# A hand-ordered attention and gated-convolution kernel: new table generation, the filter sent through the batches' own DFT, and a new order of every step

## The chip, the cores and the metric

One core of a Trainium2 chip. A core has five engines with queues of their own: TensorE (PE: matrix multiplications into PSUM, and the loads of their weights), VectorE (DVE), ScalarE (ACT), GpSimd (POOL) and SyncE (SP), which here only issues transfers. The metric is the device time of one execution in microseconds, lower is better; several runs are made and their median is taken.

## The reference, cut to what matters

Random-feature linear attention for 8 batches of 8 heads with 576 positions of 64 features; its output is a batch of 576 x 512, which goes through a gated long convolution.

```
def phi(x):
    proj = einsum('bhsd,df->bhsf', x, w_phi)              # 64 -> 128 features
    proj = proj - max(abs(proj), axis=-1, keepdims=True)
    return concatenate([exp(proj), exp(-proj)], axis=-1)
q_p, k_p = phi(q), phi(k)
kv  = einsum('bhsf,bhsd->bhfd', k_p, v);  z = sum(k_p, axis=2)
att = einsum('bhsf,bhfd->bhsd', q_p, kv) / (einsum('bhsf,bhf->bhs', q_p, z) + 1e-6)
x = att of all heads side by side                         # 8 x 576 x 512
x1, x2, x3 = split(x @ w_proj, 3)                         # 512 -> 3 * 512
x2c = irfft(rfft(x2, axis=1) * rfft(filter, axis=0), axis=1)
out = (x1 * x2c * x3) @ w_out                             # 512 -> 512
```

## The kernel before

Everything is a step, a short method of the class `Kernel`, and the order of all steps is written out by hand in the string `PLAN` (lines 26 to 186): `run` (line 997) takes its words one by one and emits each step's instructions. A word such as `Fe,ACT,0,2@6` is a step's name, its engine where it has a choice, batch and part, and the first of its PSUM banks. Every engine has its own queue and works through it strictly in the order in which the words put its instructions there; what a step needs from another engine it waits for, and everything behind it on its queue waits too. PSUM has eight banks, and a step reuses a bank as soon as its last reader is done. SBUF buffers that turn over have two to four copies (`RING`, line 22; `at`, line 216, picks the copy by an index).

The steps of a batch `b`, with `v` for a block of two heads and `X` for half of them:

- `load`, `loadh` (lines 560, 566): GpSimd issues the transfers of q, k, v into `qn`, `kn`, `vn`, cast to bf16. `trh` (line 573): SyncE issues a transposing transfer of half of it into `qT` or `kT`. For batch 0 TensorE transposes instead (`pt`, line 580) and `pte` (line 586) copies out.
- `Pk`, `Qn` (lines 597, 604), with `Pkt`, `Qnt` for the leftover positions: projections by w_phi. `maxk`, `maxq` (lines 681, 685), `maxkt`, `maxqt`: VectorE takes the maxima of the absolute values. `ex`, `exkt`, `exqt` (lines 656 to 675): ScalarE exponentiates with both signs. `mhi`, `mlo`, `trm`, `trme` prepare q's maxima as rows; `Pq`, `Pqt` (lines 628, 645) project q the other way round and subtract them.
- `em`, `vs` (lines 713, 718): v is weighted by the exponential of k's maximum, on GpSimd. `KV`, `KVe` (lines 724, 738): k's features times v, 72 matmuls a half, and the copy out. `NE`, `NEt` (lines 742, 752): q's features times that. `rc`, `xn`, `rct`, `xnt` (lines 761 to 784): VectorE divides.
- `trx`, `trxt` (lines 786, 791): SyncE issues transposing transfers of the attention output into `xT`, `xTt`; `ptx`, `ptxt` do it on TensorE for batch 0.
- `f1`, `f2` (lines 815, 821): two levels of folding by sums and differences, which make a 576-point transform into smaller ones; mostly on GpSimd. `F` (line 826): the folded DFT of the attention output by TensorE; each result has 2 x 288 columns (even and odd frequencies, cosine and sine), of which 128 + 128 go out by `Fe` (line 837) and 32 leftover ones of each by `Fet` (line 842), doubled, into `XFt`. `X2` (line 847): the middle third of w_proj is applied to the spectrum, in four chunks and a fifth for the leftover columns. `Y1`, `m3` (lines 853, 863): times the filter's spectrum (`HTe`, `HTo`, `H5`).
- `I` (line 920): the inverse transform in two halves, from which `Ie` (ScalarE copies one half), `Ip` and `Im` (VectorE sum and difference) build `cv`, and `ym` (line 973, mostly GpSimd) multiplies by the gates. `J` and `yj` (lines 957, 966) do the same with more TensorE and less elsewhere: ten matmuls instead of six, and one VectorE multiplication straight from PSUM. Before, only batch 7 uses `J`.
- `X1`, `X3` with `X1t`, `X3t` (lines 894 to 910): the outer thirds of w_proj; `X1e`, `X1te` copy X1 out, `tm`, `tmt` (lines 912, 916) multiply by X3. `yt`, `O`, `Oe`, `st` (lines 979 to 995): w_out, four row chunks a batch and a fifth for the leftovers of each pair of batches, copied by ScalarE and stored by two transfers of SyncE.

Ahead of this stand the tables. `gen_rows`, `gen_cols` (lines 345, 367) make index rows on GpSimd and index columns on VectorE; `gen_turns` (line 419) multiplies them to angles in turns on ScalarE; `gen_angles` (line 435) takes the whole turns off by a conversion to integer and a subtraction on VectorE; `gen_sin` (line 441) takes the sines. The filter is loaded by `filt_load` (line 479, four transfers of 64 KB a call), folded on one level by `filt_fold` (line 488), and transformed by `H` (line 501) with tables `D`, `D1` (a reversed `D`, by `D1m` and `D1e`) and `M5`, `M5t` (the leftover columns, copied together by `gen_five`, line 460); `H_ev` (line 514) scales the result into `HTe`, `HTo`, `H5`. `late` (line 261) ends the scratch space of the tables and allocates the later buffers in its place.

## Time and profile before

| | us |
|---|---|
| median of 3 runs | 346.66 |
| lowest, highest | 344.62, 346.82 |
| span of the profiled execution, first to last instruction | 350.6 |
| TensorE busy | 286.9 |
| VectorE busy | 263.4 |
| ScalarE busy | 225.6 |
| GpSimd busy | 225.8 |

The profiled execution's own time isn't listed apart from its span. In rows of the timeline the columns are start, duration, engine, line, operation, tiles and number; in brackets stands how long the engine was idle before it and what it waited for. Rows of groups give number, busy time, mean duration in ns of one, then the idle time before them by what ended it. The stretch view gives, for each stretch, the busy time of each engine with the number of instructions, then the granted clock of TensorE (1.00 is full), the share of the transfer engines that was busy (queues that overlap may push it over 1) and GB/s. Rows of the chain of waits give start, duration and the step that set the end there. Rows of transfer issues end with KB each and the median us from issue to landing. Matmul records are pipelined, so the mean of one is longer than its share of a row of them.

### The profile page before, as it was taken

Reading aid. Unit: us, or ns where it says so; the run is one execution under the profiler, and the core shown is the slowest. Engines: PE = TensorE matmul, PEld = TensorE weight load, DVE = VectorE, ACT = ScalarE, POOL = GpSimd, SP = SyncE. Lnnn points to the kernel's source line nnn. Section 1 sums busy time; section 2 is a strip of 40 time slices with the busy share of each in tenths; the row PEclk is TensorE's granted clock in tenths of the full one; section 3 lists DMA queues with packets and bytes.
Section 4 is the critical chain, followed back from the end, with each engine's and each line's share of the span. In section 5 each row is a group of like instructions: output and inputs, shape, how many; then the busy total and the mean of one; then the engine's idle time right before and its main releaser. Section 6 shows DMA issues by size and latency. Waiting matters only on the chain. (4 is left out here: it accounts for less than half of the span.)

```text
span 350.6 us, 10229 instructions
## 1 busy us (share of the span) xinstructions
PE 286.9 (82%) x4289; PEld 207.0 (59%) x4289; DVE 263.4 (75%) x445; ACT 225.6 (64%) x376; POOL 225.8 (64%) x191
## 2 busy tenths in 40 slices
...
GB/s 141 234 196 178 197 166 173 156 120 145 125 157 150 150 77 144 155 88 120 80 129 151 105 80 154 88 44 142 142 3 4 61 101 0 49 55 117 35 1 150
DMA packets 72030, 39.98 MB, mean 114 GB/s; under 512 B 52336, under 2 KB 66800, under 8 KB 71984
## 3 DMA queue, kind: packets, MB, share of 16 engines
...
## 5 line engine op out<-in xcount | busy, mean ns | idle before, releaser
L873 PE MATMUL ps<-xT,wproj 128*128 128x256 bf16 x512 | 63.1, 273 | 2.0 <-DMA xT<-xn 1.5
L678 DVE TENSOR_REDUCE mq<-ps 128x8 f32<-128x1024 f32 (+1 forms) x40 | 43.7, 1112 | 14.9 <-PE ps L609 7.8
L873 PEld LDWEIGHTS <-wproj 128*128 128x128 bf16 x512 | 48.0, 98 | 9.7 <-issue 2.3
L678 DVE TENSOR_REDUCE mk<-ps 128x8 f32<-128x1024 f32 (+1 forms) x40 | 43.9, 1110 | 5.1 <-ACT Ekm L664 1.3
L974 POOL TENSOR_TENSOR yT<-cv,x1s 128x576 bf16<-128x576 f32 x26 | 32.8, 1278 | 22.1 <-DVE cv L933 11.6
L865 POOL TENSOR_TENSOR T<-T,T 128x1024 bf16<-128x1024 bf16 x13 | 27.5, 2124 | 27.8 <-DVE T L861 27.8
L720 POOL TENSOR_TENSOR vm<-vn,vm 128x1152 bf16<-128x1152 bf16 x16 | 34.4, 2151 | 9.3 <-ACT vm L714 9.2
L985 PE MATMUL ps<-wout,yT 128*128 128x512 bf16 x144 | 37.0, 407 | 2.0 <-DVE xn L768 1.1
L664 ACT ACTIVATE Ekp<-ps 128x1024 bf16<-128x1024 f32 x32 | 32.6, 1027 | 9.2 <-PE ps L602 8.5
L664 ACT ACTIVATE Eqm<-ps 128x1024 bf16<-128x1024 f32 x32 | 32.6, 1035 | 8.4 <-PE ps L642 7.0
L720 POOL TENSOR_TENSOR vp<-vn,vp 128x1152 bf16<-128x1152 bf16 x16 | 34.4, 2151 | 3.1 <-ACT vp L714 3.1
L664 ACT ACTIVATE Eqp<-ps 128x1024 bf16<-128x1024 f32 x32 | 32.1, 1033 | 5.7 <-PE ps L642 5.7
L664 ACT ACTIVATE Ekm<-ps 128x1024 bf16<-128x1024 f32 x32 | 32.7, 1025 | 2.3 <-PE ps L602 2.3
L282 ACT COPY o<-ps 128x512 f32<-128x512 f32 x36 | 21.0, 588 | 20.3 <-PE ps L985 15.0
L817 POOL TENSOR_TENSOR SD<-xn 128x512 bf16<-128x512 bf16 x28 | 31.9, 1162 | 0.6 <-DVE xn L768 0.6
L926 PE MATMUL ps<-inv,T 128*128 128x288 bf16 x168 | 26.9, 306 | 4.5 <-POOL T L865 3.9
L851 PE MATMUL ps<-wproj,XF 128*128 128x512 bf16 x128 | 30.5, 380 | 0.0
L933 DVE TENSOR_TENSOR cv<-es,ps 128x288 f32<-128x288 f32 x56 | 22.4, 445 | 10.2 <-ACT es L930 5.7
L823 POOL TENSOR_TENSOR xf<-SD 128x512 bf16<-128x512 bf16 x25 | 28.3, 1153 | 0.5
L985 PEld LDWEIGHTS <-yT 128*128 128x128 bf16 x144 | 14.3, 104 | 18.7 <-issue 5.7
L914 DVE TENSOR_TENSOR x1s<-ps,x1s 128x512 bf16<-128x512 f32 x32 | 21.7, 685 | 4.5 <-PE ps L873 4.2
L749 PE MATMUL ps<-KVs,Eqp 128*128 128x65 bf16 x256 | 22.1, 201 | 1.5 <-ACT Eqm L664 1.0
...
## 6 DMA issues: line engine op xcount, KB each, us to landing
...
vn<-in_v_dram POOLq DMA_DIRECT2D x8, 576.0 KB, 10.1
qn<-in_q_dram POOLq DMA_DIRECT2D x7, 576.0 KB, 9.6
kn<-in_k_dram POOLq DMA_DIRECT2D x7, 576.0 KB, 12.4
wproj<-in_moe_w_proj_dram POOLq DMA_DIRECT2D x3, 512.0 KB, 23.0
...
```

The lines of the kernel that those rows point to most:

```text
L664: self.nc.scalar.activation(e, p, AF.Exp, bias=0.0, scale=1.0 if g == "p" else -1.0)
L678: self.nc.vector.tensor_reduce(out=out, in_=src, axis=AX.X, op=ALU.max, apply_absolute_value=True)
L720: self.eng(eng).tensor_tensor(out=t[:, :, :, 0:64], in0=self.at("vn", b)[:, 2 * X:2 * X + 2], in1=t[:, :, :, 64:65].to_broadcast([128, 2, ...
L817: self.eng(eng).tensor_tensor(out=o[:, :, 2 * i:2 * i + 2, :], in0=x[:, :, 0:2, :], in1=x[:, :, 2:4, :], op=ALU.subtract if i else ALU.add)
L823: self.eng(eng).tensor_tensor(out=o[:, :, 2 * i:2 * i + 2, :], in0=x[:, :, 0:4:2, :], in1=x[:, :, 1:4:2, :], op=ALU.subtract if i else ALU ...
L851: self.mm(self.pb(0), l, w[:, kt, 512:1024], start=(kt == 0), stop=(kt == 3))
L865: self.eng(eng).tensor_tensor(out=Y, in0=Y, in1=self.at(f"T{2 * e + 1}", b), op=ALU.add)
L873: self.mm(o[:, d], w[:, kt, f0 + 128 * m:f0 + 128 * m + 128], y[:, 1, ::-1, ::-1] if d else y[:, 0], start=(kt == 0), stop=(kt == 3))
L926: self.mm(self.pb(e, 0, 288), l, inv[:, 2 * e + i if i < 2 else 4 + e, :], start=(i == 0), stop=(i == 2))
L933: self.nc.vector.tensor_tensor(out=self.at("cv", 4 * b + m)[:, :, odd, :], in0=self.at("es", 4 * b + m).rearrange("p (x t) -> p x t", t=32 ...
L974: self.eng(eng).tensor_tensor(out=self.at("yT", b)[:, m, 0:SEQ], in0=self.at("cv", 4 * b + m).rearrange("p x h t -> p (x h t)"), in1=self. ...
L985: self.mm(self.pb(0), y[:, kt, 128 * c:128 * c + 128], w[:, kt, :], start=(kt == 0), stop=(kt == 3))
```

## The change

- **Angles.** Index rows and columns are made by other, fewer instructions (`gi_nr`, `gi_part`, `gi_fr`, `cols_i`, `cols_m`, `cols_h`, `cols_f`). `ang` computes the angles in turns plus 256 on VectorE, so that the low 15 bits of the float's mantissa are the fraction of a turn; `frac` takes them out by two shifts on the integer view; `sin` reads the integers with a scale of 2 pi / 2^15.
- **Filter.** It is loaded by eight transfers of 128 KB (`fl_load`), folded on two levels on VectorE (`fa`, then `fb` with the rows reversed by two fp32 matmuls, `rev`), transformed by `Ff` in the way of a batch's `F`, scaled by `Ffe`, and transposed by `H`, now 20 matmuls with the identity; `Hl` gathers its leftover columns. `He` takes the place of `H_ev`, in part on ScalarE. `D1`, `M5`, `M5t`, `gen_five` and `whole` are gone.
- **Leftover columns of the batches.** `Fe` copies all 2 x 288 columns of an `F`; `Fet` is gone, and one `Xl` a batch gathers and doubles the leftovers of all four blocks.
- **Buffers.** `turn_of` gives out ring copies in the order of first use, so that parts of a batch can come in any order.
- **Counts.** 22 `I` and 10 `J` (28 and 4 before), the `J` spread over the batches. Of 32 `X1e` 27 are on ScalarE (13 before); of 36 `Oe` 25 (all before), the others on VectorE; `f1` and `f2` have 25 and 23 on GpSimd (28 and 25), `ym` 21 (26). One block of batch 1 too is transposed by TensorE (`ptx`), and batch 0's leftovers go through a transposing transfer (`trxt`), no longer through TensorE.
- **Order.** All words of `PLAN` stand in a new order. The transfers of q, k, v and the weights have other places on GpSimd's queue: q and k of batch 0 come first, two thirds of w_proj, w_out, q of batch 2 and v of batches 1 and 2 after the first steps of batch 0. The stores are issued one by one (`st` has an engine and a half now), and four of batch 7's by ScalarE.

The diff, cut to its core; of `PLAN` the lines that the prediction speaks of.

```diff
-zeros gen_rows filt_loadt filt_load,1 filt_load,0 loadh,q,0,1 gen_cols loadh,q,0,0 w_load,phi
...
-Pq,1,3@4 Ip,0,0@2 Im,0,0@2 ex,q,m,1,3@4 trh,q,3,1 Im,0,1@0 NE,1,1@2 ym,POOL,0,0 rc,1,0@6 xn,1,0@6
-I,0,2@0 ex,q,p,1,3@4 rc,1,1@2 trx,1,0 xn,1,1@2 KV,2,0@6 Ie,0,2@0 ym,POOL,0,1 Ip,0,2@0 Im,0,2@0
-trx,1,1 Qnt,3@2 I,0,3@4 KVe,ACT,2,0@6 load,q,5 maxqt,3@2 ym,DVE,0,2 Pkt,3@6 Ie,0,3@4 NE,1,3@2
...
-X1,7,3@6 yj,7,1@4 X1e,ACT,7,3@6 X3,7,3@7 tm,7,3@7 J,7,3@4 yj,7,3@4 yt,DVE,7 O,7,0@4 O,7,2@5
-Oe,ACT,7,0@4 O,7,1@7 st,7,0 Oe,ACT,7,2@5 O,7,3@4 st,7,2 Oe,ACT,7,1@7 O,7,4@5 Oe,ACT,7,3@4 st,7,1
-Oe,ACT,7,4@5 st,7,3 st,7,4
...
+fl_load,1,0 loadh,q,0,0 fl_load,3,0 gi_nr loadh,q,0,1 fl_load,2,1 fl_load,0,1 gi_part gi_fr cols_i
+fl_load,2,0 w_load,phi fl_load,1,1 loadh,k,0,1 fl_load,0,0 ang,2 fl_load,3,1 cols_m loadh,k,0,0
+cols_h ang,3 fl_loadt load,v,0 frac,3 load,q,1 frac,2 gi_back load,k,1 ident sin,2 cols_f
...
+Pk,1,0@0 ptxe,DVE,0,0@4 Qn,1,1@2 trxt,0 w_load,proj,1 f1,DVE,0,0,0 X1,0,0@4 ex,k,m,1,1@6 maxk,1,1@6
...
+Pkt,1@0 X3,0,3@5 ex,k,m,1,3@6 f1,POOL,0,0,1 tm,0,1@2 maxkt,1@0 X1,0,3@4 exkt,p,1@0 load,q,2
...
+Qn,2,1@4 load,k,3 maxq,2,3@6 J,0,0@0 w_load,out ex,q,m,1,0@2 maxq,2,1@4 Pk,2,2@6 vs,POOL,p,2,0
...
+Ip,0,3@2 vs,POOL,m,2,0 Im,0,3@2 Pqt,1@6 yj,0,1@0 exqt,p,1@6 NE,1,1@2 exqt,m,1@6 Ip,0,2@4 Pq,1,3@0
...
+ex,q,p,2,0@2 tmt,1@6 st,SP,0,3,1 f2,DVE,1,0,0 F,1,3@0 X1e,ACT,1,1@7 trh,k,3,0 F,1,0@2 Fe,ACT,1,3@0
...
+tm,1,1@2 Pqt,2@6 KVe,ACT,2,1@0 Qnt,3@4 NE,2,0@2 maxqt,3@4 exqt,m,2@6 I,1,3@0 rc,2,0@2 exqt,p,2@6
...
+J,7,3@2 Ie,7,0@4 Ip,7,1@0 Im,7,0@4 ym,POOL,7,1 Ip,7,0@4 J,7,2@0 yj,7,3@2 ym,POOL,7,0 O,6,0@2
+yj,7,2@0 yt,DVE,7 O,7,1@0 Oe,ACT,6,0@2 st,SP,6,0,0 O,7,2@1 Oe,DVE,7,1@0 st,SP,6,0,1 O,7,4@2
+st,ACT,7,1,0 st,SP,7,1,1 Oe,ACT,7,2@1 O,7,0@0 Oe,ACT,7,4@2 st,SP,7,2,1 st,ACT,7,2,0 O,7,3@1
+Oe,DVE,7,0@0 st,SP,7,4,1 st,SP,7,4,0 st,ACT,7,0,1 Oe,DVE,7,3@1 st,SP,7,0,0 st,ACT,7,3,1 st,SP,7,3,0
...
+    def turn_of(self, name, key):
+        d = self.turns.setdefault(name, {})
+        return self.bufs[name][d.setdefault(key, len(d)) % len(self.bufs[name])]
...
+    def ident(self):
+        self.nc.vector.tensor_scalar(out=self.at("ident"), in0=self.idx, scalar1=0.0,
+                                     scalar2=None, op0=ALU.is_equal)
+    def one(self):
+        v, i = self.nc.vector, self.at("ident").rearrange("p (g x) -> p g x", g=4)
+        t = self.scr.tile([128, 2, 18], BF16, name="onex")
+        v.tensor_tensor(out=t, in0=i[:, 0:2, 0:18], in1=i[:, 2:4, 0:18], op=ALU.add)
+        v.scalar_tensor_tensor(out=self.at("one"), in0=t[:, 0], scalar=-1.0, in1=t[:, 1],
+                               op0=ALU.mult, op1=ALU.subtract)
...
+    def ang(self, i):
+        v, t, col = self.nc.vector, self.turn, self.col
+        def put(o, x, c, b):
+            v.tensor_scalar(out=o, in0=x, scalar1=col(c),
+                            scalar2=col(b) if isinstance(b, int) else b, op0=ALU.mult,
+                            op1=ALU.add)
+        if i == 0:
+            o = t[:, 0:2, :].rearrange("p e (s f) -> p e s f", s=2)
+            put(o[:, :, 0, :], self.fr[:, 0], 0, WHOLE + 0.25)
+            put(o[:, :, 1, :], self.fr[:, 1], 0, WHOLE)
...
+    def frac(self, i):
+        t = self.turn.bitcast(I32)[:, self.span(i), :]
+        self.nc.vector.tensor_scalar(out=t, in0=t, scalar1=17, scalar2=17,
+                                     op0=ALU.logical_shift_left,
+                                     op1=ALU.arith_shift_right)
...
-    def gen_five(self, eng):
-        e = self.eng(eng)
-        M, Mt = self.M5, self.M5t
-        e.memset(M, 0.0)
...
+    def fl_load(self, i, a):
+        self.nc.sync.dma_start(
+            out=self.fl[32 * i:32 * i + 32, 2 * a:2 * a + 2, :],
+            in_=self.dram["filt"][288 * a:288 * a + 288].rearrange(
+                "(t j) d -> t j d", j=9)[:, i:i + 6:5, :])
...
+    def fa(self, eng, i):
+        self.eng(eng).tensor_tensor(out=self.fs[:, 2 * i:2 * i + 2, :], in0=self.fl[:, 0:4:3, :],
+                                    in1=self.fl[:, 2:0:-1, :],
+                                    op=ALU.subtract if i else ALU.add)
+    def back(self):
+        self.bk = self.scr.tile([128, 128], FP32, name="bk")
+        self.nc.vector.tensor_scalar(out=self.bk, in0=self.idx2, scalar1=127.0, scalar2=None,
+                                     op0=ALU.is_equal)
+    def rev(self):
+        for i in range(2):
+            self.mm(self.pb(i), self.bk, self.fs[:, 1 + 2 * i, :], True, True)
+    def fb(self, i):
+        self.nc.vector.tensor_tensor(out=self.fe[:, 2 * i:2 * i + 2, :],
+                                     in0=self.fs[:, 0:4:2, :], in1=self.db(),
+                                     op=ALU.subtract if i else ALU.add)
+    def Ff(self, v):
+        D, Dt, c = self.at("D"), self.at("Dt"), slice(128 * v, 128 * v + 128)
+        for e in range(2):
+            self.mm(self.pb(e, 0, 288), self.f5[:, c], Dt[0:64, 0, 288 * e:288 * e + 288],
+                    start=True, stop=False)
+        for e in range(2):
+            for s in range(2):
+                self.mm(self.pb(e, 144 * s, 144 * s + 144), self.fe[:, 2 * s + e, c],
+                        D[:, 288 * e + 144 * s:288 * e + 144 * s + 144], start=False,
+                        stop=(s == 1))
+    def Ffe(self, eng, v):
+        src, dst = self.db(288), self.HF[:, v]
+        if eng == "ACT":
+            self.nc.scalar.mul(dst, src, HS)
+        else:
+            self.nc.vector.tensor_scalar(out=dst, in0=src, scalar1=HS, scalar2=None,
+                                         op0=ALU.mult)
+    def Hl(self, eng):
+        src = self.HF[:, :, :, 128:160].rearrange("p v e (s x) -> p v e s x", s=2)
+        for d in range(2):
+            for e in range(2):
+                dst = self.HL[:, :, d, e].rearrange("p v (s x) -> p v s x", s=2)
+                self.copy(eng, dst, src[:, :, e, ::-1] if d else src[:, :, e])
...
     def H(self, t):
-        D, D1, Dt, fe = self.at("D"), self.D1, self.at("Dt"), self.fe
-        if t < 4:
-            e = 2 * (t // 2)
-            c = self.cols4(t)
-            ks = [(D[:, c], fe[:, e, :]), (D1[:, c], fe[:, e + 1, :]), (Dt[:, 0, c], self.f5)]
-        else:
-            M = self.M5
-            ks = [(M[:, i % 2, 128 * (i // 2):128 * (i // 2) + 128], fe[:, i, :])
-                  for i in range(4)] + [(self.M5t, self.f5)]
-        for i, (l, r) in enumerate(ks):
-            self.mm(self.pb(0), l, r, start=(i == 0), stop=(i == len(ks) - 1))
-    def H_ev(self, eng, t):
...
+        for v in range(4):
+            l = self.main_chunk(self.HF[:, v], t) if t < 4 else self.HL[:, v].rearrange(
+                "p d e x -> p (d e x)")
+            self.mm(self.pb(0, 128 * v, 128 * v + 128), l, self.at("ident"), True, True)
...
+    def He(self, eng, t, part):
...
     def Fe(self, eng, b, v):
-        src = self.ps[:, self.bank:self.bank + 2, 0:320].rearrange("p e (s x) -> p e s x", s=2)
-        self.copy(eng, self.at("XF", b)[:, v].rearrange("p (e s) x -> p e s x", e=2),
-                  src[:, :, :, 0:128])
-    def Fet(self, eng, b, v):
-        src = self.ps[:, self.bank:self.bank + 2, 128:160].rearrange("p e (d x) -> p d e x", d=1)
-        self.copy(eng, self.at("XFt", b)[:, v].rearrange("p (d e x) -> p d e x", d=2, e=2),
-                  src.to_broadcast([128, 2, 2, 32]))
+        self.copy(eng, self.at("XF", b)[:, v], self.db(288))
+    def Xl(self, eng, b):
+        src = self.at("XF", b)[:, :, :, 128:160].rearrange("p v e (d x) -> p v d e x", d=1)
+        self.copy(eng, self.at("XL", b), src.to_broadcast([128, 4, 2, 2, 32]))
+    def main_chunk(self, x, c):
+        return x[:, c // 2, 160 * (c % 2):160 * (c % 2) + 128]
     def X2(self, b, c):
         XF, w = self.at("XF", b), self.at("wproj")
         for kt in range(4):
-            l = XF[:, kt, c, :] if c < 4 else self.at("XFt", b)[:, kt, :]
+            l = self.main_chunk(XF[:, kt], c) if c < 4 else self.at("XL", b)[:, kt].rearrange(
+                "p d e x -> p (d e x)")
             self.mm(self.pb(0), l, w[:, kt, 512:1024], start=(kt == 0), stop=(kt == 3))
...
-    def st(self, b, c):
-        o = self.at("o", 5 * b + c)
-        for i in range(2):
-            bb, j = (b, (0, 2, 5, 7)[c] + i) if c < 4 else (b - 1 + i, 4)
-            self.nc.sync.dma_start(out=self.out[bb][j:SEQ:9, :], in_=o[64 * i:64 * i + 64, :])
+        self.copy(eng, self.turn_of("o", (b, c)), self.pb(0))
+    def st(self, eng, b, c, i):
+        o = self.turn_of("o", (b, c))
+        bb, j = (b, (0, 2, 5, 7)[c] + i) if c < 4 else (b - 1 + i, 4)
+        dict(SP=self.nc.sync, ACT=self.nc.scalar)[eng].dma_start(
+            out=self.out[bb][j:SEQ:9, :], in_=o[64 * i:64 * i + 64, :])
...
-        self.whole = s.tile([128, 9, 288], I32, name="whole")
+        self.fs = self.turn.rearrange("p a x -> p (a x)")[:, 0:2048].rearrange(
-        self.f5 = s.tile([128, 512], BF16, name="f5")
-        self.D1 = s.tile([128, 576], BF16, name="D1")
-        self.M5 = s.tile([128, 2, 384], BF16, name="M5")
-        self.M5t = s.tile([128, 128], BF16, name="M5t")
+        self.f5 = s.tile([64, 512], BF16, name="f5")
+        self.HF = s.tile([128, 4, 2, 288], BF16, name="HF")
+        self.HL = s.tile([128, 4, 2, 2, 32], BF16, name="HL")
...
```

640 lines of the change are left out of this document (293 added, 347 removed).

## The prediction

> **What bounds the kernel now.** I read the run in stages and cut it where each batch starts NEt, the step at line 758 that every batch runs once, when its KV is done. The stretch view gives engine busy time, granted clock and DMA share per stage; the first row ends at batch 0's NEt, the last begins at batch 7's.
>
> ```profile
> core 0: us, PE busy (x) PEld busy (x) DVE busy (x) ACT busy (x) POOL busy (x), PEclk, DMA share, GB/s
> 0.00:52.33 52.33, 23.73 (x403) 16.73 (x403) 37.75 (x90) 36.09 (x54) 34.26 (x50) 1.00 1.15 185
> 52.33:83.75 31.42, 27.38 (x479) 21.30 (x478) 28.35 (x38) 25.81 (x44) 22.82 (x19) 0.95 1.28 150
> 83.75:133.90 50.15, 40.71 (x592) 30.14 (x592) 34.98 (x64) 27.35 (x45) 30.38 (x24) 0.90 0.92 136
> 133.90:170.27 36.37, 34.10 (x496) 24.03 (x495) 26.99 (x41) 23.54 (x42) 26.78 (x20) 0.91 0.68 120
> 170.27:206.54 36.27, 33.13 (x546) 24.25 (x543) 30.60 (x50) 24.78 (x42) 29.48 (x22) 1.00 0.64 113
> 206.54:242.03 35.49, 33.56 (x533) 23.91 (x530) 28.43 (x48) 26.43 (x45) 25.33 (x20) 1.00 0.60 102
> 242.03:276.08 34.05, 31.70 (x522) 23.22 (x519) 30.62 (x46) 24.80 (x43) 28.46 (x21) 1.00 0.25 55
> 276.08:307.38 31.30, 29.75 (x469) 21.40 (x469) 24.86 (x38) 24.18 (x43) 23.57 (x18) 1.00 0.26 57
> 307.38:350.60 43.22, 32.87 (x274) 22.05 (x273) 20.83 (x37) 12.66 (x24) 4.67 (x4) 0.91 0.31 71
> ```
>
> From 170.27 to 307.38 TensorE is busy 128.1 of 137.1 us and idles 2.2 us a stage: it is the bound there, and reordering can win little. The waste stands elsewhere: the start (TensorE 23.7 of 52.3), the stage from 83.75 (50.15 us, 9.4 idle, clock 0.90) and the end (43.22, 10.4 idle, 0.91). Next I asked the timeline for the start, on VectorE, ScalarE and VectorE again.
>
> ```profile
> 12.19 0.23 DVE L558 CAST wphi<-phi 128x128 bf16<-128x128 f32 x1 [8.29 <-DMA phi<-in_w_phi_dram]
> 3.57 0.33 DVE L379 TENSOR_SCALAR cols<-fb 128x1 f32<-128x1 f32 x4
> 18.47 4.08 DVE L678 TENSOR_REDUCE mq<-ps 128x8 f32<-128x1024 f32 x4
> 25.45 3.76 DVE L473 COPY M<-D 128x64 bf16<-128x64 bf16 x2 [0.51 <-ACT kT L282]
> 44.80 0.21 DVE L763 RECIPROCAL r<-ps 128x8 f32<-128x8 f32 x1 [0.75 <-PE ps L749]
> 17.47 1.28 ACT L453 ACT_TABLE_LOAD   x1 [5.07 <-DVE turn L439]
> ```
>
> VectorE sets the start. It waits 8.29 us for the w_phi load with the angle arithmetic queued behind, ScalarE's sines wait 5.07 for that, and from 12.2 it works almost without a pause to the first attention output (the reciprocal at 44.80). Then the two long waits, each with its clock:
>
> ```profile
> 96.77 0.29 PE L617 MATMUL ps<-wphi,qT 64*128 64x128 bf16 x2 [3.74 <-DMA qT<-qn]
> 94.21 1.99 SPq L573 DMA_TRANSPOSE qT<-qn  x1
> 98.00:102.00 4.00, 4.00 (x50) 2.89 (x50) 3.67 (x6) 1.49 (x3) 2.33 (x3) 0.50 0.78 108
> 312.75 1.03 PE L882 MATMUL ps<-xTt,wproj 128*128 128x64 bf16 x16 [2.96 <-DMA xTt<-xnt]
> 310.00:320.00 10.00, 7.25 (x49) 3.88 (x50) 4.64 (x12) 3.90 (x6) 0.00 (x0) 0.66 0.22 48
> ```
>
> At 96.77 Qnt of batch 3 waits for a transpose of q that SyncE issues only at 94.21: it overwrites the qT buffer that Pq of batch 1 has just read. At 312.75 X1t of batch 7 waits for the transpose of xnt. After each the granted clock is halved for a while (0.50 at 98 to 102; 0.66 over 310 to 320), so a wait costs more than its own length.
>
> **The change, on TensorE.** The chain of waits gives steps at full clock: four projections, five X2, two KV, one I, one J, one O.
>
> ```profile
> 328.60 3.49 PE ps L873 x32
> 324.28 4.32 PE ps L851 x20
> 300.14 2.30 PE ps L735 x144
> 303.05 0.74 PE ps L926 x6
> 337.51 1.24 PE ps L964 x10
> 304.28 0.86 PE ps L985 x4
> ```
>
> So a projection (X1 or X3) is 0.87, X2 0.86, KV 1.15, I 0.74, J 1.24, O 0.86. Six I become J: 6 x 0.50 = +3.0 us. The rest of the per-batch matmuls keep number and shape. I added these steps (and the smaller ones alike) along both orders, cut at the NEts. Before, stage by stage: 15.5, 23.5, 35.0, 30.1, 30.7, 31.1, 29.9, 28.5, 29.6. After: 18.4, 28.1, 33.5, 33.3, 29.3, 31.2, 28.3, 27.6, 29.2. The four undisturbed stages before sum to 120.2 against a measured 128.1 busy, a factor 1.066.
>
> **On the other engines.** Groups that price the rest:
>
> ```profile
> L678 DVE TENSOR_REDUCE mq<-ps 128x8 f32<-128x1024 f32 x32 | 38.8, 1219 | 9.1 <-PE ps L609 7.8 <-ACT o L282 1.2
> L439 DVE TENSOR_TENSOR turn<-turn,whole 128x864 f32<-128x864 f32 x1 | 1.1, 1059 | 0.0
> L282 ACT CAST XFt<-ps 128x128 bf16<-128x128 f32 x23 | 6.2, 268 | 8.5 <-PE ps L833 8.5
> L282 ACT CAST XF<-ps 128x512 bf16<-128x512 f32 x24 | 14.0, 589 | 2.1 <-PE ps L833 2.0
> L974 POOL TENSOR_TENSOR yT<-cv,x1s 128x576 bf16<-128x576 f32 x26 | 32.8, 1278 | 22.1 <-DVE cv L933 11.6 <-PE ps L749 5.2 <-DVE r L763 3.0
> L930 ACT COPY es<-ps 128x288 f32<-128x288 f32 x28 | 11.2, 404 | 13.0 <-PE ps L926 12.1 <-ACT es L930 0.8
> L933 DVE TENSOR_TENSOR cv<-es,ps 128x288 f32<-128x288 f32 x56 | 22.4, 445 | 10.2 <-ACT es L930 5.7 <-PE ps L926 2.1 <-POOL yT L974 1.9
> L512 PE MATMUL ps<-fe,D 128*128 128x512 bf16 x8 | 3.3, 505 | 0.0
> ```
>
> Fet goes 32 times (ACT 6.2 us; the nine on VectorE at about the same price 2.5); eight Xl come. Xl has no row: 512 elements a partition lie between Fet's 0.27 and the exponentials' 1.0; I take 0.59, the copy of as many elements. Fe now carries 576 elements instead of 512: 0.59 to 0.66, no more. Six I less: Ie -2.4 on ACT, Ip and Im -5.3 on VectorE, five ym less on POOL -6.4; six yj +4.3 on VectorE (576 elements at the 1.23 ns an element of the L439 row). X1e moves 14 copies from VectorE to ACT, Oe eleven the other way: three more on ACT, +1.8, and three fewer on VectorE. POOL loses the filter folds and the table masks besides, some 24 us in all. None of this stands on the path except where these engines bind, that is at the start and in stage 52.33 to 83.75; in the undisturbed stages TensorE's 31 us cover it.
>
> **Start.** POOL now issues two half loads of q ahead of the column index, so VectorE begins at about 3.1 instead of 1.0. Then 30 column operations (0.08 each by the row at 3.57), eleven angle rows of 144 or 288 elements (0.08 as a floor; the L439 row's rate gives 0.18 and 0.35, which I take), four frac on 576 or 864 integers (the same rate gives 0.71 and 1.06 as upper bounds; I take 0.65 and 0.95, one source being less) and copies bring it to w_phi at 14; w_phi no longer holds the angles back. ScalarE's sines and copies, from 9 on, deliver the first q transposes for Qn at 16, so the first maximum falls at 16.4, not 18.47. From there VectorE's list up to the first reciprocal is ten maxima at 1.22, fa and fb 4 x 1.25 (1024 elements at that rate), two maxima of half the width 1.4, Hl as four short copies 1.2, five He at half a maximum and a little, 3.4, and small ones: 24.7 us. M5's copies (3.76 for two of them) and D1 are gone. One wait is new: fb needs rev, two matmuls on fp32 data that the trace doesn't show. Their lower bound is the bf16 row of the same shape, 0.5 each; as upper bound, both operands being twice as wide, I take four times that, 2.0 each. VectorE has 1.7 us of other work meanwhile, so the wait is 0 to 2.3; I take 1.7, behind which the maxima of k queue. That gives the reciprocal at 42.8, and 5.5 us of list later NEt at 48. The range is 45 to 52.
>
> The Trainium skill, "FP8 and Floating Point Precision", section TensorE Precision Notes, states that true FP32 takes four passes through the array. By it the wait would be the upper 2.3 and the start 0.6 us later; no run here shows it yet.
>
> **Middle.** For each batch I measured TensorE's work between the last reader of a qT half and its next first user. Batch 3: 7.1 and 2.4 us before (the stall above), 18.2 and 24.9 after. From NEt to X1t: 1.8 to 10.1 before, 7.5 to 20.3 after; batch 7, 1.9 before, 16.3 after. So both transposes above get time to land, and with the waits go the half clocks behind them. NE to X1, which waits for xT the same way, stays at 3.4 to 6.0 (3.0 to 6.7 before; batch 0 uses TensorE). Every stage then costs its work x 1.066 plus 2.2 idle: 37.9, 37.7, 33.5, 35.5, 32.4, 31.7 for the six stages from batch 1's NEt on. In the stage ahead of them TensorE would give 32.2, but ACT (35.1 counted), VectorE (33.9) and POOL (32.5) are now as full, each about 30 in measured terms; chained to each other they add: I take 36, between 32 and 42.
>
> **Loads.** They leave POOL's queue later. Two wproj thirds, wout, q2, v1 and v2 were issued in the crowded start and now follow f1 and vs on that queue, which wait for VectorE.
>
> ```profile
> wproj<-in_moe_w_proj_dram POOLq DMA_DIRECT2D x3, 512.0 KB, 23.0
> qn<-in_q_dram POOLq DMA_DIRECT2D x7, 576.0 KB, 9.6
> ```
>
> The 23.0 belongs to a start with DMA share 1.15. With fewer loads ahead I take 9.6. The wproj third for X2 is issued near 49 and needed at 48 + 11.3 x 1.3 = 63; q2 is issued near 54 and its Qn is due near 71, with two transposes between. Both just fit, at no cost; priced otherwise under the rivals.
>
> **End.** Stores are split in halves and four of the last ten are issued by ScalarE.
>
> ```profile
> 339.58 4.48 PE L985 MATMUL ps<-wout,yT 128*128 128x512 bf16 x20 [0.85 <-DVE yT L968]
> 320.73 26.79 SPq L995 DMA_DIRECT2D out_dram<-o  x16
> 299.38 1.11 SPq L995 DMA_DIRECT2D out_dram<-o  x2
> ```
>
> The last matmul ends at 344.06, SyncE issues until 347.52, all ends at 350.6. After: one copy 0.6, one issue 0.56, 3.1 to land and close, 0.4 of handovers: 4.7 instead of 6.5. The last stage is 29.2 x 1.066 + 2.2 + 4.7 = 38 (43.22 before), since the wait at 312.75 and its half clock are gone; the last ym on POOL hides behind J and O of batch 6.
>
> **Sum.** 48 + 36 + 37.9 + 37.7 + 33.5 + 35.5 + 32.4 + 31.7 + 38 = 330.7 against the span of 350.6: -19.9. By stage: -4.3, +4.6, -12.2, +1.3, -2.8, 0, -1.7, +0.4, -5.2. The page names no other time of the profiled execution than its span, which is 3.9 above the median of 346.66; scaled by 0.943 the median becomes 327.
>
> **Rivals.** *Waits move* (faster, but little): the stage from batch 1's NEt and the next one keep half of the 14 us that the long stage lost beyond the rule, at new places, and the start gains nothing: 330.7 + 7 + 4 = 342 in span, 338 as a median. For: four engines are equally full there, and both long waits quoted were followed by a low clock. Against: the named waits have visible causes, and these are undone.
>
> *Late loads* (slower): the deferred loads land as wproj did, 23.0 after issue. Then X2 of batch 0 waits 9 us, Qn of batch 2 about 9, vs of batch 2 (v2 is listed only 5.4 us of TensorE work ahead of it) and wout at O of batch 0 some 5 more, each with 1.7 of half clock: 330.7 + 30 = 361 in span, 357 as a median. It beats the old time once these waits sum to over 20 us, that is with landings over about 20 us. Against: the queue has less ahead of it.
>
> *No difference*: the new order wastes what the old did in total, with J's 3 us on top of the gains at start and end: 345.
>
> A rule of the Trainium skill ("TensorE: Matmul & The Clock Gate", What's actually happening) says that the clock halves after an idle window of about 3.4 us; the 3.74 us wait fits. By it many shorter waits would leave the clock alone, which lends the first rival less.
>
> **Chances.** Forecast 0.61 (range 317 to 335), waits move 0.20, no difference 0.07, late loads 0.12. Start (45 to 52), the full stage (32 to 42) and idle per stage (1.6 to 3.1 over seven) give the inner range; with the first rival the outer is 317 to 343. A change under 1% (3.5 us) can't be told from none. Faster 0.81, same 0.07, slower 0.12.
>
> **What would show it.** Right: the first NEt at 45 to 52, no DMA wait over 2 us on TensorE between 80 and 140, no xTt wait near the end, a clock of 1.00 in most stages, the 6.5 us behind the last matmul down to 4.7. Wrong: TensorE waiting for wproj, qT or vs in the second and third stage, or a first NEt beyond 52 behind rev.

## The result, and the profile after

The changed kernel takes 362.86 us (median of four runs, 360.56 to 367.82), the kernel before in the same series 346.74: a ratio of 1.044 (95% interval 1.036 to 1.052). It is slower; forecast were 327.0 and a range of 317 to 343. Medians here are of all executions of a kernel, while the ratios leave out those more than 1.5% above its fastest, so the two can differ by a few us. The profiled execution of the changed kernel took 361.55 us with a span of 359.8, so 1.8 lie outside the span.

This is the stretch view of the changed kernel, cut at the NEt of each batch (line 778 now), as the prediction cut the kernel before.

```profile
core 0: us, PE busy (x) PEld busy (x) DVE busy (x) ACT busy (x) POOL busy (x), PEclk, DMA share, GB/s
0.00:57.89 57.89, 30.17 (x455) 21.79 (x456) 45.80 (x99) 32.91 (x50) 18.34 (x28) 0.82 0.70 122
57.89:94.03 36.14, 31.56 (x528) 24.00 (x528) 31.47 (x43) 30.63 (x51) 32.33 (x26) 1.00 0.88 143
94.03:137.49 43.46, 37.77 (x557) 26.95 (x553) 27.88 (x49) 25.43 (x39) 20.82 (x16) 0.92 0.72 117
137.49:175.10 37.61, 35.21 (x540) 24.98 (x539) 31.19 (x46) 27.02 (x45) 28.09 (x22) 1.00 0.82 133
175.10:211.81 36.71, 31.46 (x516) 23.43 (x515) 31.40 (x44) 22.01 (x35) 23.94 (x17) 1.00 0.96 147
211.81:249.15 37.34, 33.38 (x523) 23.95 (x521) 28.76 (x43) 26.43 (x44) 25.36 (x20) 1.00 0.80 121
249.15:290.69 41.54, 32.68 (x511) 23.77 (x511) 31.71 (x45) 23.39 (x39) 19.20 (x13) 0.92 0.29 56
290.69:324.10 33.41, 30.17 (x485) 21.39 (x485) 26.82 (x43) 23.62 (x38) 21.25 (x15) 0.95 0.31 59
324.10:359.80 35.70, 29.93 (x244) 20.45 (x241) 23.58 (x40) 8.63 (x18) 14.10 (x11) 0.97 0.38 95
```

Beside the prediction, stage by stage (the last column is a version from the experiments below):

| stage | before | predicted | changed kernel | g1 |
|---|---|---|---|---|
| start to batch 0's NEt | 52.3 | 48 | 57.9 | 52.8 |
| from NEt 0 | 31.4 | 36 | 36.1 | 36.0 |
| from NEt 1 | 50.1 | 37.9 | 43.5 | 37.7 |
| from NEt 2 | 36.4 | 37.7 | 37.6 | 37.3 |
| from NEt 3 | 36.3 | 33.5 | 36.7 | 34.9 |
| from NEt 4 | 35.5 | 35.5 | 37.3 | 36.5 |
| from NEt 5 | 34.1 | 32.4 | 41.5 | 35.4 |
| from NEt 6 | 31.3 | 31.7 | 33.4 | 31.1 |
| from NEt 7 to the end | 43.2 | 38 | 35.7 | 35.0 |
| sum | 350.6 | 330.7 | 359.8 | 336.7 |

The misses stand in few places: 9.9 us in the start, 5.6 and 9.1 in the two stages with a clock of 0.92, and 1.7 to 3.2 in three stages at 33 to 37. Of the whole 29.1, these six make 31.3; the end gives 2.3 back.

**The start.** The timeline shows it on VectorE, with GpSimd and TensorE beside it (start, duration, engine, line, operation).

```profile
37.11 8.42 DVE L296 COPY HL<-HF 128x128 bf16<-128x128 bf16 x4
39.01 2.16 POOL L740 TENSOR_TENSOR vp<-vn,vp 128x1152 bf16<-128x1152 bf16 x1
46.18 0.37 PE L656 MATMUL ps<-qT,wphi 64*128 64x256 bf16 x1 [5.76 <-DVE HTo L296]
52.23 0.21 DVE L783 RECIPROCAL r<-ps 128x8 f32<-128x8 f32 x1
```

The four short copies Hl, priced at 1.2 us, take 8.42 and end with the last of the four products vs of 2.15 us that GpSimd runs from 36.09 to 45.37. VectorE's He queue behind them, and TensorE waits 5.76 us for a bank. The copies are far from equal. The view of the tile HL gives the shortest, median and longest in ns, then the first and the last start: first all four, then the two long ones alone.

```profile
L296 DVE COPY HL<-HF x4: 180/682/7119, 37.1 to 45.3; 128x128 bf16<-128x128 bf16 x4
L296 DVE COPY HL<-HF x1: 1184/1184/1184, 37.1 to 37.1; 128x128 bf16<-128x128 bf16 x1
L296 DVE COPY HL<-HF x1: 7119/7119/7119, 38.3 to 38.3; 128x128 bf16<-128x128 bf16 x1
```

Two take 0.18 us. One, begun beside the first product, takes 1.18 and ends with it. One, begun at 38.3, while GpSimd issues a transfer between its first and second product, takes 7.12: it waits through all three products that are left.

**The two long stages.** The timeline on TensorE and the two queues at the longest wait, then the stretch view for the clock behind it and at two more places.

```profile
250.91 0.81 POOL L581 DMA_DIRECT2D vn<-in_v_dram  x1
251.18 1.24 SPq L807 DMA_TRANSPOSE xT<-xn  x1
258.73 1.23 PE L894 MATMUL ps<-xT,wproj 128*128 128x256 bf16 x5 [6.61 <-DMA xT<-xn]
106.02 0.59 PE L894 MATMUL ps<-xT,wproj 128*128 128x256 bf16 x2 [2.93 <-DMA xT<-xn]
```

```profile
27.00:40.00 13.00, 8.37 (x77) 5.31 (x78) 10.70 (x12) 9.96 (x17) 4.87 (x5) 0.50 0.32 43
105.00:109.00 4.00, 2.50 (x12) 1.58 (x12) 0.00 (x0) 0.43 (x1) 0.00 (x0) 0.52 1.28 185
255.50:261.50 6.00, 2.77 (x10) 1.35 (x10) 0.00 (x0) 0.59 (x1) 0.00 (x0) 0.50 0.94 205
```

The transposing transfer of xn for X1 of batch 5 is issued at 251.18, a quarter of a microsecond behind the load of v for batch 6, and lands 7.5 us later; the one issued before it, at 249.23, took 2.5. For X1 of batch 1 the loads of k and q of batch 4 stand at the same place. The clock is halved after both waits.

**The middle.** The groups of k's maxima and exponentials in the changed kernel, kept apart by shape (count, busy, mean ns, idle before them by releaser):

```profile
L698 DVE TENSOR_REDUCE mk<-ps 128x8 f32<-128x1024 f32 x32 | 39.1, 1221 | 18.1 <-ACT Ekp L684 10.3 <-ACT Ekm L684 7.2 <-PE ps L622 0.6
L684 ACT ACTIVATE Ekm<-ps 128x1024 bf16<-128x1024 f32 x32 | 32.9, 1034 | 10.4 <-DVE mk L698 9.0 <-PE ps L622 1.4
L684 ACT ACTIVATE Ekp<-ps 128x1024 bf16<-128x1024 f32 x32 | 32.6, 1033 | 10.3 <-DVE mk L698 6.7 <-PE ps L622 3.5
```

ScalarE waits 15.7 us for maxima and VectorE 17.5 for exponentials: the three readers of one pair of banks take turns. In the new order the maximum stands between the two exponentials for 16 of the 32 blocks, before for 9, and there the same two groups hardly waited for each other:

```profile
L664 ACT ACTIVATE Ekm<-ps 128x1024 bf16<-128x1024 f32 x32 | 32.7, 1025 | 2.3 <-PE ps L602 2.3
L678 DVE TENSOR_REDUCE mk<-ps 128x8 f32<-128x1024 f32 x32 | 38.7, 1217 | 3.1 <-ACT Ekm L664 1.3 <-PE ps L602 1.1 <-ACT o L282 0.4
```

### The profile page after: what moved, and what is told of

It reads as the page before. It is cut to its first block, busy times and chain, and to the rows that moved or that the text cites. A ratio compares the mean times of both kernels' runs of the same rounds, so it can differ in the third digit from the quotient of the medians.

```text
span 359.8 us, 10234 instructions
## 1 busy us (share of the span) xinstructions
PE 292.3 (81%) x4344; PEld 210.7 (59%) x4344; DVE 278.6 (77%) x446; ACT 220.1 (61%) x350; POOL 203.4 (57%) x163
## 4 chain that ended last, share of the span: by engine, by line
PE 40%; DVE 12%; DMA 10%; ACT 10%; issue 5%; POOL 2%; SPq 1%; DVEq 0%; POOLq 0%; ACTq 0%
PE ps L894 8%; PE ps L872 7%; DVE mk L698 5%; DMA xT<-xn 4%; ACT Ekm L684 3%; PE ps L1010 3%; PE ps L769 3%; PE ps L947 3%; DMA kT<-kn 3%; PE ps L755 3%; ACT Ekp L684 3%; DMA kn<-in_k_dram 2%; PE ps L656 2%; PE ps L989 2%; PE ps L849 2%
## 5 line engine op out<-in xcount | busy, mean ns | idle before, releaser
L894 PE MATMUL ps<-xT,wproj 128*128 128x256 bf16 x512 | 66.5, 280 | 12.2 <-DMA xT<-xn 10.9
L894 PEld LDWEIGHTS <-wproj 128*128 128x128 bf16 x512 | 49.7, 100 | 23.5 <-issue 14.4
L740 POOL TENSOR_TENSOR vm<-vn,vm 128x1152 bf16<-128x1152 bf16 x15 | 32.2, 2149 | 26.5 <-ACT vm L734 26.5
L999 POOL TENSOR_TENSOR yT<-cv,x1s 128x576 bf16<-128x576 f32 x21 | 26.6, 1278 | 32.0 <-DVE cv L954 28.2
L740 POOL TENSOR_TENSOR vp<-vn,vp 128x1152 bf16<-128x1152 bf16 x16 | 34.4, 2152 | 15.9 <-ACT vp L734 12.7
L837 POOL TENSOR_TENSOR SD<-xn 128x512 bf16<-128x512 bf16 x25 | 28.7, 1163 | 20.7 <-DVE xn L788 17.4
L1010 PE MATMUL ps<-wout,yT 128*128 128x512 bf16 x144 | 36.5, 389 | 0.5 <-ACT o L294 0.4
L886 POOL TENSOR_TENSOR T<-T,T 128x1024 bf16<-128x1024 bf16 x13 | 27.6, 2126 | 13.6 <-DVE T L882 13.6
L294 ACT CAST x1s<-ps 128x512 bf16<-128x512 f32 (+1 forms) x32 | 17.4, 560 | 26.6 <-PE ps L894 19.5
L882 DVE TENSOR_TENSOR T<-ps,HTe 128x1024 bf16<-128x1024 f32 x16 | 19.0, 1216 | 13.1 <-PE ps L872 12.9
L656 PE MATMUL ps<-qT,wphi 64*128 64x256 bf16 x128 | 17.1, 279 | 9.0 <-DVE HTo L296 5.8
L788 DVE TENSOR_TENSOR xn<-ps,r 128x512 bf16<-128x512 f32 x32 | 22.0, 689 | 0.9
L769 PE MATMUL ps<-KVs,Eqp 128*128 128x65 bf16 x256 | 20.3, 193 | 2.9 <-issue 0.9
```

Source lines behind the costliest of these rows:

```text
L656: self.mm(o[:, d], w[r, :], y, start=True, stop=False)
L740: self.eng(eng).tensor_tensor(out=t[:, :, :, 0:64], in0=self.at("vn", b)[:, 2 * X:2 * X + 2], in1=t[:, :, :, 64:65].to_broadcast([128, 2, ...
L769: self.mm(self.pb(u, 65 * a, 65 * a + 65), E, KVs[:, u, v, s, :], start=(s == 0), stop=(s == 1))
L837: self.eng(eng).tensor_tensor(out=o[:, :, 2 * i:2 * i + 2, :], in0=x[:, :, 0:2, :], in1=x[:, :, 2:4, :], op=ALU.subtract if i else ALU.add)
L886: self.eng(eng).tensor_tensor(out=Y, in0=Y, in1=self.at(f"T{2 * e + 1}", b), op=ALU.add)
L894: self.mm(o[:, d], w[:, kt, f0 + 128 * m:f0 + 128 * m + 128], y[:, 1, ::-1, ::-1] if d else y[:, 0], start=(kt == 0), stop=(kt == 3))
```

## The experiments

In the first four kernels below (labels with e) the end of `PLAN` is not that of the changed kernel: the steps from `Ie,7,0` to `st,ACT,7,1,0` are missing (in the last of them from `tm,7,0` to `Oe,ACT,7,4`), and the steps behind them stand two or more times. So of these four only what lies ahead of batch 7's NEt is read; their total times are those of kernels with another end. All later kernels are whole.

**Hl on ScalarE (e1).**

```diff
-Pq,0,1@4 trh,k,1,0 Hl,DVE em,p,0,1 em,m,0,1
+Pq,0,1@4 trh,k,1,0 Hl,ACT em,p,0,1 em,m,0,1
```

> The changed kernel, but ScalarE makes the four small copies of the filter's leftover columns (Hl) instead of VectorE. Theory A (VectorE's SBUF-to-SBUF copies each wait for the GpSimd product that runs beside them; in the changed kernel they take 8.42 us and TensorE then waits 5.76 us for HTo): the four copies take under 2 us in all on ScalarE, the 5.76 us wait shrinks below 1 us, the first NEt falls at 50 to 53 instead of 57.89, and the time drops by 5 to 7 us, to 356 to 358. Theory B (the start is bound by the length of the engines' lists, and the wait only shows which of them came last): TensorE waits elsewhere, the first NEt stays within 2 us of 57.89, and the time drops by less than 2 us.

**Hl on VectorE, GpSimd's products later (e1b).**

```diff
-trm,0@0 em,m,0,0 ex,k,m,0,3@4 vs,POOL,m,0,0 Ffe,DVE,2@6 trme,ACT,0@0 em,p,0,0 exkt,p,0@2
-Pq,0,1@4 trh,k,1,0 Hl,DVE em,p,0,1 em,m,0,1
+trm,0@0 ex,k,m,0,3@4 Ffe,DVE,2@6 trme,ACT,0@0 exkt,p,0@2 em,m,0,0 vs,POOL,m,0,0 em,p,0,0
+em,p,0,1 em,m,0,1 Pq,0,1@4 trh,k,1,0 Hl,DVE
```

> The changed kernel with the four copies Hl left on VectorE, but the four exponentials that release GpSimd's products of batch 0 (em) come some 2.5 us later on ScalarE's queue, so that VectorE's copies run while GpSimd stands still. Theory A (the copies wait for GpSimd): four copies of about 0.2 us, 1 us in all instead of 8.42, first NEt at 50 to 53, the time down by 5 to 7 us, as with the copies on ScalarE. A rival (the copies are slow in themselves, by their reversed or short rows): they take 8 us again, and nothing is gained. If only the place on the queue matters, no copy changes its length.

Measured: the first NEt at 53.9 and 54.0 us instead of 57.9 (totals, with the other end, 359.87 and 363.01 us; ratio of the first 1.031, 1.020 to 1.043). From the timeline of the one with Hl on ScalarE, then of the other:

```profile
38.75 0.89 ACT L294 COPY HL<-HF 128x128 bf16<-128x128 bf16 x4
75.37 0.29 PE L637 MATMUL ps<-wphi,kT 64*128 64x128 bf16 x2 [3.88 <-DMA kT<-kn]
```

```profile
37.85 0.50 DVE L296 COPY HL<-HF 128x128 bf16<-128x128 bf16 x4
42.41 0.69 DVE L296 CAST HTe<-ps 128x512 bf16<-128x512 f32 x1 [1.92 <-ACT HTe L537]
205.40 0.39 PE L637 MATMUL ps<-wphi,kT 64*128 64x128 bf16 x4 [5.54 <-DMA kT<-kn]
```

The same four copies take 0.50 us on VectorE while GpSimd stands still, here and in the whole kernels f4 and g1 below: they are not slow in themselves, and beside the products they wait. The start gains 3.9 us, and the first NEt misses the 50 to 53 expected. A new wait of 1.92 us for ScalarE's HTe appears on VectorE, but it is not what holds the start: g3 below removes it and gains nothing. Batch 7's NEt hardly follows (323.4 and 325.1 against 324.1), because each of the two kernels meets a wait for kT, 3.88 us where the changed kernel has none and 5.54 where it has 1.82, again a transposing transfer among loads.

**Three loads moved (e2, and whole f2).**

```diff
-em,m,2,1 load,k,4
...
-X1,1,1@7 load,q,4
...
+vs,POOL,p,2,1 load,k,4
...
+m3,POOL,1,0 load,q,4
...
+O,3,4@1 load,k,7 load,v,6
...
-ex,k,m,6,2@2 load,v,6
```

> The changed kernel with three loads moved on GpSimd's queue: v of batch 6 earlier by some 24 us (behind k of batch 7), k of batch 4 and q of batch 4 later by 10 to 20 us. Theory C (in the changed kernel a load issued just ahead of a transposing transfer of xn takes the transfer engines from it, so X1 of batch 5 waits 6.61 us and X1 of batch 1 2.93 us, and half clock follows): both waits shrink below 1 us, stage 249.15 to 290.69 becomes 33 to 35 us instead of 41.5, the stage before 137.5 about 3 us shorter, and the time drops by 8 to 11 us, to 352 to 355. Rival (the transposing transfers are slow because the transfers of q, k and the stores on SyncE's own queue stand around them): the 6.61 us wait keeps over 4 us, and the time drops by less than 3 us.

> The changed kernel, whole, with the three loads moved (v of batch 6 earlier; k and q of batch 4 later). Theory C (loads take the transfer engines from the transposes of xn) from the run of the same move before: xT waits 2 to 3 us in all instead of 10.9, the stage from batch 1's NEt 38 us and the one from batch 5's 36 us (43.5 and 41.5 in the changed kernel), time 349 to 355 us. Rival: the stages fall as said but what they gain is waited for elsewhere, and the time stays at 359 to 364 us.

Measured, the whole kernel: 348.19 us (ratio to before 1.007, 1.002 to 1.012), 14.7 below the changed kernel and so beyond what either expectation gave. The first of the two, with the other end, took 352.99 (352 to 355 expected); in its profile the stage from NEt 0 took 42.7 us instead of 36.1, with waits of 2.13 and 2.10 for kT and qT, though its order up to there is the changed kernel's. From the whole one's stretch view, the two stages, and its longest remaining wait for xT:

```profile
94.60:132.20 37.60, 35.02 (x556) 25.46 (x553) 27.87 (x49) 25.08 (x39) 20.80 (x16) 1.00 0.79 136
244.10:278.90 34.80, 31.15 (x511) 23.08 (x511) 31.56 (x45) 23.22 (x39) 18.40 (x12) 1.00 0.23 49
```

```profile
248.34 0.71 PE L894 MATMUL ps<-xT,wproj 128*128 128x256 bf16 x5 [1.61 <-DMA xT<-xn]
```

The stages fall by 5.9 and 6.7 us and run at full clock: a wait and the half clock behind it go together. The rival (SyncE's own transfers) falls, since these stay where they were. By the two ratios (1.044 and 1.007) the gain is 12.7 us, which is what the two stages give.

**k's maxima behind the pair of exponentials (e3, and whole f3).** Thirteen maxima move, after this pattern:

```diff
-ex,k,p,5,0@4 maxk,5,0@4 f1,POOL,4,0,1 O,3,3@0 ex,k,m,5,0@4
+ex,k,p,5,0@4 f1,POOL,4,0,1 O,3,3@0 ex,k,m,5,0@4 maxk,5,0@4
```

> The changed kernel with 13 of k's maxima (batches 2 to 7) moved behind the second of the two exponentials that read the same PSUM banks; nothing else moves. Theory D (exponential, maximum, exponential on the same banks hand over between ScalarE and VectorE twice, each waits for the other, and TensorE waits for the banks): the idle of the k exponentials for the maximum (9.0 and 6.7 us) and of the maxima for the exponentials (17.5 us) halve, and the time drops by 3 to 6 us. Rival (these engines have time to spare in the middle, so their waits cost nothing; the stages are long because TensorE waits for other things): within 1.5 us of the changed kernel.

> The changed kernel, whole, with 13 of k's maxima moved behind the second exponential. Theory D, from the middle stages of the run of the same move before (from batch 0's NEt to batch 7's 260.0 us against 266.2): the time drops by 4 to 7 us, to 356 to 359 us, and ScalarE's k exponentials wait 6 us in all for the maxima instead of 16. Rival: the 6 us of that run were another sequence of clock drops, and the time stays within 2 us of 362.9.

Measured: the one with the other end 362.98 us, the whole one 355.14 (ratio 1.029, 1.021 to 1.037; 356 to 359 expected), 7.7 less than the changed kernel by the medians and 5.1 by the ratios. Groups of the whole one:

```profile
L684 ACT ACTIVATE Ekm<-ps 128x1024 bf16<-128x1024 f32 x32 | 32.9, 1039 | 2.7 <-DVE mk L698 1.5 <-PE ps L622 1.2
L684 ACT ACTIVATE Ekp<-ps 128x1024 bf16<-128x1024 f32 x32 | 32.8, 1036 | 11.7 <-PE ps L622 5.5 <-DVE mk L698 4.0 <-DVE xf L843 2.2
```

ScalarE's wait for maxima falls from 15.7 to 5.5 us, as expected. VectorE's for exponentials does not halve: it goes from 17.5 to 18.7 us. And the 7.7 us are not all the move's worth: in this profile the stage from NEt 5 is 4.6 us shorter because the load of v for batch 6 comes at 252.99, behind the transpose of 251.16, which then lands in 2.5 us. Cleaner is the profile of the kernel below with all three moves beside the one with only the loads moved: the four stages from NEt 3 to the last NEt take 136.6 us against 142.0. The stage from NEt 2 takes 40.0 against 37.4 there (and 40.3 in this kernel, 37.6 in the changed one): for k's maxima of batches 3 and 4 the move costs about half of what the later ones gain. Which of them costs it was not tried.

**All three together (f4), and the kernel before once more (f5).**

> The changed kernel with all three: the exponentials that release GpSimd's products behind the four copies Hl, the three loads moved, k's maxima behind the pairs. If the three causes are separate their gains add: -4 (start), -9 (loads), -5 (maxima) from 362.9: 344 to 347 us, level with the kernel before (0.99 to 1.01 of it). If they are one chain, in which each gain is only waited for at the next place, the time is that of the best of them alone, 350 to 354 us (1.01 to 1.02).

> The kernel before, unchanged, for a second profile: the first one's span of 350.6 lies above its median. Both theories: a span of 343 to 347; the question is which stages of the first profile were longer than usual, and whether the clock drops stand at the same places.

Measured: 345.87 us, ratio 0.994 (0.990 to 0.999). The gains do not quite add, and one place shows why. Timeline and stretch view:

```profile
73.50 0.29 PE L637 MATMUL ps<-wphi,kT 64*128 64x128 bf16 x2 [3.33 <-DMA kT<-kn]
```

```profile
52.70:94.30 41.60, 33.69 (x526) 24.91 (x526) 31.63 (x43) 30.85 (x50) 32.31 (x26) 0.92 1.01 128
71.00:77.00 6.00, 3.27 (x50) 1.80 (x52) 2.04 (x3) 2.41 (x4) 5.87 (x4) 0.57 0.61 85
```

The first NEt is at 52.7, 5.2 us sooner than in the changed kernel, but the next stage is 5.5 longer: TensorE comes to Pkt of batch 2 before k's transpose, and the low clock follows. That need not come with the shorter start: the kernel with Hl before the products had no such wait (stage 36.7), and the first kernel with the loads moved had it with the old start. So this place is close, and its wait comes in some executions only; the twelve of this kernel lie between 341.05 and 355.64.

The kernel before gave a profiled execution of 352.36 us, against a median of 346.2 over its timed runs in that series, and a span of 350.6 instead of the 343 to 347 expected. Both profiled executions of it have this span, some 6 us above what is usual for it. So its stage table is that of a long execution, and the stages show 9.2 us of loss where the medians show 16.1. The two do not agree stage by stage: from NEt 0 the second takes 35.8 us instead of 31.4, from NEt 1 46.6 instead of 50.1, with low clocks at partly other places, so single stages of it move by some 4 us. Which stages are shorter in its usual executions was not seen.

**Loads of batch 1 early (g2).** To f4, three loads are added ahead of an f1 for which GpSimd's queue waits 11.8 us in the changed kernel and 3.97 in f4 itself.

```diff
+NEt,0@2 load,v,1 w_load,proj,1 load,q,2 f1,POOL,0,1,1
...
-xnt,0,0@2 load,v,1
...
-trxt,0 w_load,proj,1
...
-exkt,p,1@0 load,q,2
```

> The kernel with the three causes undone (345.87 us) and three loads moved as well: v of batch 1, the third of w_proj and q of batch 2 ahead of the first f1 on GpSimd's queue, which stands idle for 11.8 us before it while the transfer engines stand idle too. Theory E (what the start gains is lost in the next stage, where these deferred loads fill the transfer engines and k's transpose for batch 2 comes late, a wait of 3.33 us with 6.8 us of half clock behind it): the stage from batch 0's NEt falls from 41.7 to 35 to 37 us, the time by 4 to 6 us, to 340 to 342. Rival (the transposes of k are late because SyncE issues them late, behind xTt): the wait stays over 2 us and the time within 1.5 us of 345.9.

Measured: 342.68 us, ratio 0.990 (0.986 to 0.994), 3.2 us less by the medians and 1.5 by the ratios, whose intervals overlap (4 to 6 expected). The stage goes as expected, and it stays at 36.0 to 36.2 in the three kernels after this one; by the stretch view of this kernel, which also shows the middle of its start:

```profile
54.20:90.30 36.10, 31.41 (x528) 23.94 (x527) 31.35 (x43) 30.59 (x51) 30.02 (x23) 1.00 0.95 137
27.00:40.00 13.00, 8.28 (x76) 5.27 (x76) 9.22 (x14) 9.56 (x17) 1.91 (x3) 1.00 0.30 42
```

**Loads spread, maxima moved only for batches 5 to 7 (g1).**

```diff
+load,v,4 load,k,5
...
-em,p,4,0 load,k,5
...
-Qn,5,0@4 load,q,7
...
+f2,POOL,4,1,0 load,q,7
```

> As the run with early loads of batch 1, but k's maxima moved only for batches 5 to 7 (for batches 3 and 4 the move made the stage from batch 2's NEt 2.6 us longer), and k of batch 5 loaded earlier and q of batch 7 later, away from the transposes. If these stages go back as they were: 2 to 4 us less than that run, 337 to 339 us, 0.975 to 0.98 of the kernel before. If the stages only exchange their waits: no less than that run, within 1 us.

Measured: 340.74 us (338.52 to 342.58), ratio 0.984 (0.979 to 0.989): 2 us less than the run before it as expected, though not the 337 to 339, and 21 (ratios) to 22 (medians) less than the changed kernel. It is 1.6% faster than the kernel before. Its stretch view from batch 0's NEt to batch 7's:

```profile
0.00:52.80 52.80, 29.25 (x456) 20.57 (x457) 38.00 (x99) 32.84 (x50) 20.54 (x31) 0.87 0.76 133
52.80:88.80 36.00, 31.50 (x527) 23.96 (x527) 31.33 (x43) 30.49 (x50) 29.99 (x23) 1.00 0.95 143
88.80:126.50 37.70, 35.06 (x558) 25.51 (x555) 27.91 (x49) 25.16 (x39) 20.84 (x16) 1.00 0.77 134
235.20:270.60 35.40, 31.45 (x511) 23.27 (x511) 32.42 (x45) 23.20 (x39) 19.13 (x13) 1.00 0.21 44
```

Every stage between the start and the end runs at full clock; the four rows stand for nine, of which the table above has the lengths.

**One hand-over less in the start (g3, from g1).**

```diff
-He,ACT,0,1@7 He,DVE,0,0@7
+He,DVE,0,0@7 He,ACT,0,1@7
```

> As the spread kernel, with VectorE's He of the first transform chunk ahead of ScalarE's on the bank that both read. Theory F (the start still holds hand-overs on one bank: VectorE waits 1.92 us for ScalarE's HTe, TensorE 1.8 us for VectorE's): first NEt 1 to 2 us sooner, the time 1 to 2 us down. Rival: the first output waits for the products of GpSimd and nothing moves.

Measured: 340.58 us, ratio 0.983 (0.980 to 0.987), no different from the one before. The wait on VectorE is gone, as its timeline shows (HTe at 40.22; at 42.18, behind 1.92 us of waiting, in g1), and the first NEt stays at 53.1: theory F falls, and which chain ends last there is open.

```profile
40.22 0.68 DVE L296 CAST HTe<-ps 128x512 bf16<-128x512 f32 x1
```

**Six J made I again (g4, from g1).** Two copies of `es` are too few for three halves under way at some of these places, so a few half sums take another block's half and the output is not the reference's; the amount of work is that of the step.

```diff
-J,0,0@0
+I,0,0@0 Ie,0,0@0
...
-yj,0,0@0
+Ip,0,0@0 Im,0,0@0 ym,POOL,0,0
```

> As the spread kernel, with six of the ten J made I again (six matmuls instead of ten on TensorE; six copies more on ScalarE, six times two half sums instead of one product on VectorE, six products more on GpSimd), so as many as in the kernel before. By the prediction's term (J costs TensorE 0.50 us more, nothing else is on the path): 3 us less than the spread kernel. Rival (in batches 0 to 3, VectorE and ScalarE are as full as TensorE; VectorE gets some 0.2 us and ScalarE 0.4 more for each): within 1 us, or up to 3 us more.

Measured: 346.88 us, ratio 1.002 (0.999 to 1.006): 6.1 us more than with the J, more than the rival said. From its stretch view and VectorE's groups:

```profile
90.40:129.00 38.60, 34.28 (x547) 24.51 (x544) 28.07 (x51) 25.60 (x40) 25.72 (x20) 1.00 0.80 135
167.30:206.10 38.80, 33.44 (x511) 23.95 (x510) 31.46 (x45) 22.14 (x36) 24.00 (x17) 0.93 0.63 116
```

TensorE is busy 0.8 us less than in the row of 88.80 above, and the stage is 0.9 longer. The stage from NEt 3 alone is 3.9 us longer, with a low clock (0.93) whose cause was not followed up. Shown is that J was no cost to the whole; that its shorter chain through the other engines is worth more than its 0.50 us on TensorE is argued, not shown.

## Why the prediction was wrong, point by point

- **Start, the step that prices Hl "as four short copies 1.2".** Measured 8.42: 7.2 of the 9.9 us. The quoted row of two copies M with 3.76 us (one took 3.67, the other 0.17) showed a short SBUF copy on VectorE that took many times its length, and it was used as work removed, not as a price for the same kind of operation beside GpSimd. The Trainium skill, "SBUF — State Buffer", section Who interferes with whom, says that VectorE's copies may take both port pairs, one of which GpSimd shares, and that the engine that comes second "fully blocks" while the first has the pair. The runs agree in that the copies wait: 8.42 us, against 0.50 with the products moved. But the copy of 7.12 us began before the three products that it waited through, so in this trace a waiting copy did not come in between products that follow each other.
- **Start, the list of 24.7 us with one wait of 1.7.** The list began 1.3 us sooner than said (15.10 against 16.4). The wait for rev was 1.78, close to a 1.7 that was picked within 0 to 2.3; in g1 it was 2.08. But VectorE waits for the exponentials and for banks besides: with rev's, seven waits make 5.4 us between 15.1 and 52.2 in the changed kernel, and eight make 8.2 in g1, where Hl no longer fills that time. The sum is -1.3 + 7.2 + 3.7 (5.4 less the 1.7 counted) = 9.6 us, and the reciprocal was 9.4 late (52.23 against 42.8). The remaining rows:

```profile
15.10 1.23 DVE L698 TENSOR_REDUCE mq<-ps 128x8 f32<-128x1024 f32 x1 [1.84 <-PE ps L629]
23.73 2.35 DVE L493 TENSOR_TENSOR fe<-turn,ps 128x1024 bf16<-128x1024 f32 x2 [1.78 <-PE ps L490]
```

- **Middle, "NE to X1 ... stays at 3.4 to 6.0" of TensorE's work.** The count of work was right, its use not: whether a transfer has time to land was asked of TensorE's order alone, and not of what else the transfer engines have in hand at that moment. The two stages lost 5.6 and 9.1 us, of which moving three loads gave back 5.9 and 6.7.
- **Loads "at no cost".** The loads themselves landed in time, by the changed kernel's rows of transfer issues, so the rival "late loads" as written did not come. It named the wrong victim: the loads hit the transposes.

```profile
qn<-in_q_dram POOLq DMA_DIRECT2D x7, 576.0 KB, 9.8
wproj<-in_moe_w_proj_dram POOLq DMA_DIRECT2D x3, 512.0 KB, 5.4
```

  In f4 the same happened in the stage from NEt 0, by 5.5 us, which three earlier loads gave back.
- **Each stage "its work x 1.066 plus 2.2 idle".** About right where nothing collides: g1's eight stages after the start sum to 283.9 us against 282.7 predicted. In part that is luck: the first seven take 4.2 us more than said, and the end 3.0 less. In the changed kernel the place of k's maxima, which the sum puts at nothing, cost some 5 us in the stages from NEt 3 on.
- **J "+3.0".** TensorE's own price was about right (0.8 us for two J, by the rows above), the price for the whole had the wrong sign: taking six out made the kernel 6.1 us slower.
- **What was right.** The waits for qT and xTt over 2 us are gone, and with the latter the low clock behind it; the end took 35.7 us against 38 (behind the last matmul 5.4 us are left, and not 4.7). The stage from NEt 2 took 37.6 against 37.7, the one from NEt 0 36.1 against 36, a value picked between 32 and 42.
- **A rival's sum.** In "waits move", the long stage lost not 14 us beyond the rule but 10.6 (50.15 less 35.0 x 1.066 + 2.2 = 39.5), which makes that rival 340 us in span. Its picture, waits that come back at new places, is nearest to what happened, but the start did not stay as it was: it lost 5.6 us.
- **The scale.** Measured against its own median, a profiled execution of the kernel before is long; by the span and 1.8 us outside it, as in the changed kernel, the sum of 330.7 would have been 332.5 and not 327. Of the 35.9 us between 327.0 and 362.86 the stages are 29.1, this scale is 5.5, and 1.3 is the distance of the profiled execution from the median.

So three kinds of collision (GpSimd's products beside VectorE's copies, loads ahead of transposes, readers of one pair of banks in turns) cost 21 to 22 us. Without them the order is worth 6.2 us against the kernel before (346.94 beside g1), and not the 19.7 forecast: of the 13.7 us from 327.0 to g1's 340.74, 5.5 are the scale, 6.0 the stages, 4.8 of them in the start, and 2.2 the distance of g1's profiled execution from its median.
